# Fourier pieces placed in pairs between two feed-forward units, the second in a bank of u and v

## The chip, the cores and the metric

The kernel runs on one core of a Trainium2 chip. The metric is device time in microseconds (us) for one launch; the time before is the median of three runs. One further run was profiled, and every instruction time below is from that execution, counted from the start of its span.

## What is computed

```python
X = np.fft.fft(x, axis=1)          # x: 8 x 3008 x 256
X = np.fft.fft(X, axis=2)
x = X.real.reshape(8 * 3008, 256)
h = x @ w_in                       # 256 -> 2048
g = np.where(h >= 1, h, np.where(h <= -1, 0, (h + 1) ** 2 / 4))
return g @ w_out                   # 2048 -> 256
```

The weights arrive as 64-bit floats, so the kernel also converts them on the chip, at its start.

## The kernel before

The eight batches are taken one after the other. The 3008 points of a batch are 47 times 64, so its transform along the first axis is done in two stages of small matmuls. The transform along the second axis is folded into `w_in`. Because the input is real, outputs come in mirrored pairs, and the kernel computes for each pair two sums u and v, whose sum and difference are the two hidden values.

**Units.** The feed-forward part of a batch is 48 units: 3 chunks of up to 512 columns (482 in the first chunk) times 16 slices of the 2048 hidden features. `units` lists them; below, r is the number of a unit in its batch, 0 to 47. A unit i has two halves:

- `gemm1(i)`: three matmuls into a first bank (u) and three into a second (v), all on L344. Then VectorE forms `us` from u (L347), which is the last reader of u's bank, and `h = us - v` and `h = us + v` (L349, L350), which are the only readers of v's bank. Then come two ScalarE passes `a` (L353, L354), a VectorE pass over `h` (L355), a ScalarE rounding `gh` (L358) and two GpSimd differences `gl` (L360).
- `gemm2(i)`: twelve matmuls into four accumulators (L385) from `gh` and `gl`. It is issued `LAG` = 4 units behind `gemm1`. At the last slice of a chunk the accumulators are copied out by VectorE (L397) and ScalarE (L395), and the next chunk reuses the same four banks.

**PSUM.** The eight banks have fixed tags: four `acc`, three `uv` and one `fft`. A unit takes two `uv` banks, so three banks turn round: unit i has a and b, unit i+1 has c and a, unit i+2 has b and c.

**Pieces.** While batch b runs its 48 units, the transform of batch b+1 is done in 15 pieces: eight of `stage1` (L267: eight matmul records of 96 columns, the first piece two more from L270), one `nyquist` (L282: two records) and six of `stage2` (L303: eight records of 128 columns). Every piece writes a bank from `fft_bank`, which is the one bank with the tag `fft` (for batch 0, before the loop, the accumulators' banks are used instead). The bank is free again when it has been copied out: by four ScalarE copies `z` for `stage1` (L275), by ScalarE and VectorE (L169, L170) for `stage2`. `stage1` of piece q needs `y`, a GpSimd sum of two halves of the input (L131), with three buffers.

**Where pieces stand.** The loop over units calls `gemm1(i)`, then possibly a piece, then `gemm2(i - LAG)`. A piece is due when the share of the work done has fallen behind the share of units passed (`done < total * ...`), and in any case at the first slice of a chunk (`change`). It is held back one unit before such a change (`soon`). From batch 1 on this puts the 15 pieces behind the units r = 0, 4, 6, 9, 13, 16, 20, 23 (`stage1`), 26 (`nyquist`), 28, 31, 34, 36, 41 and 44 (`stage2`). For batch 0 they stand between r = 25 and 46. The last batch has none.

**Order.** Tile buffers and semaphores come from the framework. Its scheduler lays down, when the kernel is built, one fixed order of instructions for each engine. That order starts from the program's, but an instruction whose buffer or input is not expected in time is passed by others.

Of the kernel before, what the change touches and what calls it, by code (L numbers as in the profile page):

```python
# [9 lines left out]
F32 = mybir.dt.float32  # L10
# [12 lines left out]
P = 128  # L23
XC = 8
GPC = 4
CH = 512
# [83 lines left out]
def fft_ffn_kernel(ctx: ExitStack, tc: tile.TileContext, x, cst, w_in, w_out, out):  # L110
# [5 lines left out]
    ps = ctx.enter_context(tc.tile_pool(name="ps", bufs=1, space=bass.MemoryType.PSUM))  # L116
# [3 lines left out]
    def load_x(b, q):  # L120
        tag, bufs = ("xt", 4) if b or q < 4 else ("gl", 4) if q < 7 else ("o", 2)
        t = sb.tile([96, 2, CH], F32, tag=tag, name=f"x_{b}_{q}", bufs=bufs)
        nc.sync.dma_start(t, x[b, q])
        xt[b, q] = t
# [31 lines left out]
    def load_cm():  # L156
        nc.sync.dma_start(cm, cst[:, _OFF[3] :])

    early = [0]

    def fft_bank(b, name):

        if b == 0 and early[0] < EARLY_BANKS:
            early[0] += 1
            return ps.tile([P, CH], F32, tag=f"acc{early[0] % 4}", name=name, bufs=1)
        return ps.tile([P, CH], F32, tag="fft", name=name, bufs=1)

    def split(hi, lo, src):
# [23 lines left out]
    def convert_w(n):  # L192
# [3 lines left out]
        if n in CV:  # L196
            tag, bufs = CV[n]
            t = sb.tile([P, 2, CH], U32, tag=tag, name=f"cv_{n}", bufs=bufs)
            man, exp = t[:, 0], t[:, 1]
            lowf, shifted = low.bitcast(F32), exp  # L200
        else:
            if n % 2 == 0:
                f32s["pair"] = sb.tile([P, 2, CH], U32, tag="xt", name=f"cv_{n}", bufs=4)
            man, exp = f32s["pair"][:, n % 2], high
            lowf = fft_bank(1, f"cps_{n}")
            shifted = lowf.bitcast(U32)
# [28 lines left out]
    def fold_bank(f4, name):  # L235
        if f4 < 2:
            return fft_bank(0, name)
        return ps.tile([P, CH], F32, tag="uv", name=name, bufs=3)
# [69 lines left out]
    def fft_pieces(b):  # L308
        pieces = []
        for q in range(XC):  # L310
            pieces.append((4, lambda q=q: stage1(b, q)))
        pieces.append((2, lambda: nyquist(b)))
        for h in range(NC // 4):
            pieces.append((4, lambda h=h: stage2(b, h)))
        return pieces
# [19 lines left out]
    def gemm1(i):  # L335
        b, k, f, *_ = units[i]
        n = WIDTH[k]
        hi, lo = pq[b, k]
        cols = slice(f * P, (f + 1) * P)
        uv = []  # L340
        for m in range(2):
            t = ps.tile([P, CH], F32, tag="uv", name=f"uv_{i}_{m}", bufs=3)
            for j, (w, r) in enumerate(((wh, hi), (wl, hi), (wh, lo))):
                nc.tensor.matmul(t[:, :n], w[m][:, cols], r[:, m, :n], start=(j == 0), stop=(j == 2))  # L344
            uv.append(t[:, :n])
        us = sb.tile([P, CH], F32, tag="us", name=f"us_{i}", bufs=2)[:, :n]
        nc.vector.scalar_tensor_tensor(us, nyb[b, k][:, :n], delta[:, f : f + 1], uv[0], op0=ALU.mult, op1=ALU.add)  # L347
        h = sb.tile([P, 2, CH], F32, tag="h", name=f"h_{i}", bufs=3)[:, :, :n]
        nc.vector.tensor_tensor(h[:, 0], us, uv[1], op=ALU.subtract)  # L349
        nc.vector.tensor_tensor(h[:, 1], us, uv[1], op=ALU.add)  # L350
        a = sb.tile([P, 2, CH], F32, tag="a", name=f"a_{i}", bufs=3)[:, :, :n]

        nc.scalar.activation(a, h, AF.Relu, bias=half, scale=0.5)  # L353
        nc.scalar.activation(a, a, AF.Square)  # L354
        nc.vector.scalar_tensor_tensor(h, a, 1.0, h, op0=ALU.min, op1=ALU.max)  # L355
        gh = sb.tile([P, 2, CH], F32R, tag="gh", name=f"gh_{i}", bufs=4)[:, :, :n]
        gl = sb.tile([P, 2, CH], F32R, tag="gl", name=f"gl_{i}", bufs=4)[:, :, :n]
        nc.scalar.activation(gh, h, AF.Copy)  # L358
        for sg in range(2):
            nc.gpsimd.tensor_tensor(gl[:, sg], h[:, sg], gh[:, sg].bitcast(F32), op=ALU.subtract)  # L360
        acts[i] = gh, gl

    accs = []
    per = NCHUNK * NFT
    n_units = NB * per

    def gemm2(i):
        b, k, f, first, last, (v, visits) = units[i]
        n = WIDTH[k]
        gh, gl = acts.pop(i)  # L370
        if first:
            accs[:] = [ps.tile([P, CH], F32, tag=f"acc{j}", name=f"acc_{i}_{j}", bufs=1) for j in range(4)]
            if v:

                outs[k] = new_o(i)
                for dh in range(2):
                    nc.sync.dma_start(outs[k][dh][:, :, :n], parts[k][dh, :, :, :n])
        if last:
            o = outs.pop(k) if v else new_o(i)
        for dh in range(2):  # L380
            wc = slice(dh * P, (dh + 1) * P)
            for sg in range(2):
                acc = accs[dh * 2 + sg]
                for j, (w, g) in enumerate(((woh, gh), (wol, gh), (woh, gl))):
                    nc.tensor.matmul(  # L385
                        acc[:, :n], w[:, f, wc], g[:, sg], start=(first and j == 0), stop=(last and j == 2)
                    )
                if last:

                    dst = o[dh][:, sg, :n]  # L390
                    with tc.high_priority(offset=EVICT_AHEAD):
                        if v:
                            nc.vector.tensor_tensor(dst, acc[:, :n], dst, op=ALU.add)
                        elif sg:
                            nc.scalar.activation(dst, acc[:, :n], AF.Copy)  # L395
                        else:
                            nc.vector.tensor_copy(dst, acc[:, :n])  # L397
                    if i == n_units - 1:
                        nc.sync.dma_start(out[b, k, dh, sg, :, :n], dst)
            if last and v < visits - 1:  # L400
                nc.sync.dma_start(parts[k][dh, :, :, :n], o[dh][:, :, :n])
            elif last and i < n_units - 1:
                nc.sync.dma_start(out[b, k, dh].rearrange("s p t -> p s t")[:, :, :n], o[dh][:, :, :n])
# [7 lines left out]
    n1 = XC  # L411
# [11 lines left out]
    def run_steps(names):  # L423
        for s in names.split():
            steps[s[0]](int(s[1:]))
# [3 lines left out]
    pending, done, total = [], 0, 1  # L429
    for i in range(n_units + LAG):  # L430
        run_steps(STEPS.get(i, ""))
        if i < n_units:
            b, r = divmod(i, per)
            r0 = 0 if b else FIRST_DFT
            if r == (0 if b else FIRST_LOAD) and b + 1 < NB:
                for q in range(4):
                    load_x(b + 1, q)
            if r == r0:
                pending = fft_pieces(b + 1) if b + 1 < NB else []
                done, total = 0, sum(w for w, _ in pending)  # L440
            gemm1(i)

            change = units[max(i - LAG, 0)][3]
            soon = units[max(i - LAG + 1, 0)][3]
            while pending and (change or not soon and done < total * (r + 1 - r0) / (per - r0)):
                change = False
                w, f = pending.pop(0)
                f()
                done += w
                k1 = n1 + 7 - len(pending)  # L450
                if 4 <= k1 + 3 < XC:
                    load_x(b + 1, k1 + 3)
        if i >= LAG:
            gemm2(i - LAG)

# [53 lines left out]
```

## Time and profile before

| | |
|---|---|
| median of 3 runs | 1774.29 us (1773.91 to 1776.93) |
| profiled run | 1774.87 us, of which 1773.1 us are the span of the trace |
| granted TensorE clock, mean | 0.995 |
| matmuls into `acc` / `uv` | 4608 / 2304 |
| one evacuation copy `z` on ScalarE | 339 ns, 256 of them |
| the fold `y` on GpSimd | 1789 ns, 56 of them |

The span is the time from the first to the last instruction in the trace; the run's own time lies 1.8 us above it. In the trace, PE is TensorE's matmuls, PEld its weight loads, DVE is VectorE, ACT is ScalarE and POOL is GpSimd. A matmul is in flight longer than its turn: matmuls overlap, so what a matmul costs is the distance from its start to the next start, not its duration. Each row of a timeline gives start, duration, engine, line, operation and tiles, and at its end in brackets the idle time of the engine before it and what ended it.

### The profile page before, as it was taken

What the parts mean: (1) busy time and instruction counts of PE and PEld (TensorE: products, weight loads), DVE (VectorE), ACT (ScalarE), POOL (GpSimd) and SP (SyncE); (2) the same over time, 40 slices, a digit from 0 to 9 for tenths busy, and PEclk for the clock granted to TensorE, in tenths of its full rate; (3) what the DMA queues carried; (4) which work ended last, traced back from release to release, by engine and by line L of the source; (5) the groups of instructions that cost most, each with busy time, mean ns of one, the idle gap of its engine ahead of it and who ended that gap; (6) DMA issues with size and microseconds to landing.
All of it is one profiled execution on the core that took longest, in us unless ns stands there. A gap on an engine that the chain in (4) does not pass through costs nothing.

```text
span 1773.1 us, 21990 instructions
## 1 busy us (share of the span) xinstructions
PE 1743.6 (98%) x8014; PEld 1425.2 (80%) x8014; DVE 1439.3 (81%) x1762; ACT 1345.3 (76%) x1577; POOL 1199.4 (68%) x837
## 2 busy tenths in 40 slices
PE   9998999999999999999999999999999999999998
PEld 6766788888888788887888888888888888888876
DVE  5989888888887888878878788878888788888886
ACT  4776777787777777777778877788778787777775
POOL 0545776776677767687667776677666766667766
PEclk8999999999999999999999999999999999999999
DMA  7013322010011100101001100011000000000000
GB/s 228 1 58 111 100 82 89 28 50 18 24 43 30 58 31 1 51 27 53 30 10 51 49 28 24 19 41 50 28 25 33 1 23 33 10 24 12 12 25 24
DMA packets 29964, 72.53 MB, mean 41 GB/s; under 512 B 2976, under 2 KB 8224, under 8 KB 29856
## 3 DMA queue, kind: packets, MB, share of 16 engines
q1 hardware_dynamic: 29568, 70.08, 11.9%
q8 instruction: 63, 1.03, 0.2%
q10 hardware_dynamic: 288, 1.05, 0.2%
q14 instruction: 45, 0.37, 0.1%
HBM read 43.31 MB, written 27.81 MB: 40 GB/s over the span
## 4 chain that ended last, share of the span: by engine, by line
PE 70%; ACT 11%; DVE 7%; POOL 5%; issue 5%; DMA 1%; POOLq 0%; ACTq 0%; DVEq 0%
PE acc L385 43%; PE uv L344 22%; POOL gl L360 5%; DVE h L355 5%; ACT a L354 4%; ACT gh L358 3%; ACT a L353 3%; PE s L267 2%; PE s L303 2%; ACT z L275 1%; DMA raw<-in_moe_w_in_dram 1%; PE wps L246 1%; DVE h L349 0%; DVE h L350 0%; DVE o L397 0%
## 5 line engine op out<-in xcount | busy, mean ns | idle before, releaser
L360 POOL TENSOR_TENSOR gl<-h,gh 128x512 fp32r<-128x512 f32 (+1 forms) x768 | 1099.1, 1454 | 539.6 <-ACT gh L358 517.3
L355 DVE SCALAR_TENSOR_TENSOR h<-a,h 128x1024 f32<-128x1024 f32 (+1 forms) x384 | 581.6, 1514 | 226.0 <-ACT a L354 224.4
L358 ACT ACTIVATE gh<-h 128x1024 fp32r<-128x1024 f32 (+1 forms) x384 | 400.6, 1043 | 356.3 <-DVE h L355 327.5
L385 PE MATMUL acc<-gh,woh 128*128 128x512 f32 (+1 forms) x1536 | 608.5, 397 | 7.4 <-ACT gh L358 4.1
L385 PE MATMUL acc<-gl,woh 128*128 128x512 f32 (+1 forms) x1536 | 604.7, 394 | 6.8 <-POOL gl L360 6.7
L385 PE MATMUL acc<-gh,wol 128*128 128x512 f32 (+1 forms) x1536 | 596.8, 389 | 0.5 <-DVE wol L170 0.5
L353 ACT ACTIVATE a<-h,biases 128x1024 f32<-128x1024 f32 (+1 forms) x384 | 431.6, 1124 | 12.2 <-DVE h L350 9.8
L354 ACT ACTIVATE a<-a 128x1024 f32<-128x1024 f32 (+1 forms) x384 | 398.5, 1038 | 7.1
L385 PEld LDWEIGHTS acc<-gl,woh 128*128 128x128 f32 x1536 | 288.7, 188 | 74.1 <-POOL gl L360 14.5
L385 PEld LDWEIGHTS acc<-gh,woh 128*128 128x128 f32 x1536 | 289.7, 189 | 70.7 <-ACT gh L358 6.8
L385 PEld LDWEIGHTS acc<-gh,wol 128*128 128x128 f32 x1536 | 289.8, 189 | 60.8 <-DVE wol L170 1.3
L349 DVE TENSOR_TENSOR h<-us,uv 128x512 f32<-128x512 f32 (+1 forms) x384 | 259.6, 676 | 63.3 <-POOL gl L360 22.3
L344 PE MATMUL uv<-pqh,wh 128*128 128x512 f32 (+1 forms) x768 | 303.8, 396 | 4.5 <-DVE h L350 2.7
L344 PE MATMUL uv<-pql,wh 128*128 128x512 f32 (+1 forms) x768 | 301.9, 393 | 0.0
L344 PE MATMUL uv<-pqh,wl 128*128 128x512 f32 (+1 forms) x768 | 299.7, 390 | 0.0
L347 DVE SCALAR_TENSOR_TENSOR us<-nyb,delta,uv 128x512 f32<-128x512 f32 (+1 forms) x384 | 278.7, 727 | 15.9 <-PE uv L344 15.4
L350 DVE TENSOR_TENSOR h<-us,uv 128x512 f32<-128x512 f32 (+1 forms) x384 | 256.3, 668 | 0.0
L344 PEld LDWEIGHTS uv<-pqh,wh 128*128 128x128 f32 x768 | 144.4, 188 | 43.3 <-DVE h L350 8.5
L344 PEld LDWEIGHTS uv<-pql,wh 128*128 128x128 f32 x768 | 144.7, 188 | 32.5 <-issue 0.5
L344 PEld LDWEIGHTS uv<-pqh,wl 128*128 128x128 f32 x768 | 144.5, 188 | 30.1
L131 POOL TENSOR_TENSOR y<-x 96x512 f32<-96x512 f32 x56 | 100.1, 1789 | 7.1 <-PE s L267 3.1
L275 ACT ACTIVATE z<-s 64x192 f32<-64x192 f32 x256 | 86.8, 339 | 14.0 <-PE s L267 6.7
(53 smaller groups left out, 552.5 us busy)
## 6 DMA issues: line engine op xcount, KB each, us to landing
x<-in_x_dram SPq DMA_DIRECT2D x64, 384.0 KB, 3.3
out_dram<-o SPq DMA_DIRECT2D x30, 512.0 KB, 2.8
out_dram<-o SPq DMA_DIRECT2D x16, 482.0 KB, 3.1
nyb<-nyr SPq DMA_DIRECT2D x24, 256.0 KB, 3.3
raw<-in_moe_w_out_dram SPq DMA_DIRECT2D x8, 512.0 KB, 11.7
raw<-in_moe_w_in_dram SPq DMA_DIRECT2D x6, 512.0 KB, 5.2
part<-o SPq DMA_DIRECT2D x4, 512.0 KB, 3.5
o<-part SPq DMA_DIRECT2D x4, 512.0 KB
```

What stands on the lines that cost most here:

```text
L131: nc.gpsimd.tensor_tensor(y, t[:, 0], t[:, 1], op=ALU.add)
L275: nc.scalar.activation(dst, src, AF.Copy)
L344: nc.tensor.matmul(t[:, :n], w[m][:, cols], r[:, m, :n], start=(j == 0), stop=(j == 2))
L347: nc.vector.scalar_tensor_tensor(us, nyb[b, k][:, :n], delta[:, f : f + 1], uv[0], op0=ALU.mult, op1=ALU.add)
L349: nc.vector.tensor_tensor(h[:, 0], us, uv[1], op=ALU.subtract)
L350: nc.vector.tensor_tensor(h[:, 1], us, uv[1], op=ALU.add)
L353: nc.scalar.activation(a, h, AF.Relu, bias=half, scale=0.5)
L354: nc.scalar.activation(a, a, AF.Square)
L355: nc.vector.scalar_tensor_tensor(h, a, 1.0, h, op0=ALU.min, op1=ALU.max)
L358: nc.scalar.activation(gh, h, AF.Copy)
L360: nc.gpsimd.tensor_tensor(gl[:, sg], h[:, sg], gh[:, sg].bitcast(F32), op=ALU.subtract)
L385: nc.tensor.matmul(acc[:, :n], w[:, f, wc], g[:, sg], start=(first and j == 0), stop=(last and j == 2))
```

## The change

Where one piece was due, two are now placed, one directly behind the other. `fft_bank` gives the first of the two the `fft` bank as before and the second a bank of the tag `uv`. The test for a due piece is the same, but it is asked once for a unit instead of in a loop, and a due unit places two pieces whether or not the second is due. The input loads that follow a piece go with it. The number of banks and buffers stays the same.

```diff
-    early = [0]
+    early, second = [0], [False]
...
             return ps.tile([P, CH], F32, tag=f"acc{early[0] % 4}", name=name, bufs=1)
+        if second[0]:
+            return ps.tile([P, CH], F32, tag="uv", name=name, bufs=3)
         return ps.tile([P, CH], F32, tag="fft", name=name, bufs=1)
...
-            while pending and (change or not soon and done < total * (r + 1 - r0) / (per - r0)):
-                change = False
-                w, f = pending.pop(0)
-                f()
-                done += w
-                k1 = n1 + 7 - len(pending)
-                if 4 <= k1 + 3 < XC:
-                    load_x(b + 1, k1 + 3)
+            if pending and (change or not soon and done < total * (r + 1 - r0) / (per - r0)):
+
+                for second[0] in (False, True):
+                    if pending:
+                        w, f = pending.pop(0)
+                        f()
+                        done += w
+                        k1 = n1 + 7 - len(pending)
+                        if 4 <= k1 + 3 < XC:
+                            load_x(b + 1, k1 + 3)
+                second[0] = False
```

With the weights 4, 2 and 4 of the pieces, the same test now gives pairs behind r = 0, 4, 13 and 20 (two `stage1` each), 26 (`nyquist` and the first `stage2`), 31 and 36 (two `stage2` each), and the last `stage2` alone behind r = 44. In batch 0 the pairs stand behind r = 25, 28, 31, 34, 36, 40 and 44, with the last piece behind 46.

## The prediction

> **What bounds the kernel now.** I read the page's busy times and chain of waits first.
>
> ```profile
> span 1773.1 us, 21990 instructions
> ...
> PE 1743.6 (98%) x8014; PEld 1425.2 (80%) x8014; DVE 1439.3 (81%) x1762; ACT 1345.3 (76%) x1577; POOL 1199.4 (68%) x837
> ...
> PE 70%; ACT 11%; DVE 7%; POOL 5%; issue 5%; DMA 1%; POOLq 0%; ACTq 0%; DVEq 0%
> ```
>
> TensorE is busy for 98% of the span and holds most of the chain. An average over stages says little, so next I asked for busy times by stage; the columns are the stretch, its length, then each engine's busy time.
>
> ```profile
> 100.00:200.00 100.00, 87.97 (x382) 65.59 (x381) 90.30 (x125) 73.33 (x95) 59.23 (x45) 1.00 0.29 92
> ...
> 496.00:584.00 88.00, 88.00 (x419) 74.50 (x418) 69.42 (x82) 69.09 (x89) 64.66 (x47) 1.00 0.12 39
> ...
> 285.00:1557.00 1272.00, 1270.86 (x5898) 1052.06 (x5897) 1031.79 (x1230) 988.66 (x1146) 907.72 (x627) 1.00 0.10 32
> ```
>
> From 285 to 1557 us, the steady stretch of six batches with all their pieces, the PE row shows 1.1 us of idle in 1272. The idle time of the kernel lies at its start, while weights are converted (12 us of idle between 100 and 200), and in the last batch, which has no pieces. So the change can win in the steady stretch only by making matmul turns shorter, or by removing short waits that a busy row hides. Those are in the view of waits, from 285 to 1557 us (total, times, longest), for matmuls:
>
> ```profile
> PE acc L385 <- DVE o L397: 0.8, 3, 0.3
> ```
>
> and for their weight loads, which wait in a matmul's place:
>
> ```profile
> PEld uv L344 <- DVE h L350: 3.7, 11, 0.5
> PEld acc L385 <- DVE o L397: 3.1, 5, 0.7
> PEld uv L344 <- DVE us L347: 2.3, 7, 0.4
> ```
>
> Two kinds of wait exist: 3.9 us on the copies that empty the accumulators at a change of chunk, and 6.0 us on VectorE to give back a bank of u and v. The second kind is small, but it shows that the `uv` banks are already used to the edge.
>
> **The change part by part.**
>
> *Turns of the matmuls.* No matmul is removed. What pairing can save is the passage from a piece back to the units. A `stage1` piece looks so on PE:
>
> ```profile
> 553.75 1.03 PE L267 MATMUL s<-cs,y 96*128 96x96 f32 x8
> 554.57 0.46 PE L385 MATMUL acc<-gh,woh 128*128 128x482 f32 x1
> 554.87 0.38 PE L385 MATMUL acc<-gh,wol 128*128 128x482 f32 x1
> 555.09 0.38 PE L385 MATMUL acc<-gl,woh 128*128 128x482 f32 x1
> ```
>
> A `stage2` piece, in a chunk of 512 columns:
>
> ```profile
> 435.70 1.05 PE L303 MATMUL s<-cs,z 128*128 128x128 f32 x8
> 436.51 0.48 PE L385 MATMUL acc<-gh,woh 128*128 128x512 f32 x1
> 436.82 0.39 PE L385 MATMUL acc<-gh,wol 128*128 128x512 f32 x1
> 437.05 0.39 PE L385 MATMUL acc<-gl,woh 128*128 128x512 f32 x1
> ```
>
> And `nyquist`:
>
> ```profile
> 611.65 0.31 PE L282 MATMUL ny<-cs,z 128*24 128x64 f32 x2
> 611.90 0.51 PE L385 MATMUL acc<-gh,woh 128*128 128x512 f32 x1
> 612.24 0.39 PE L385 MATMUL acc<-gh,wol 128*128 128x512 f32 x1
> ```
>
> The `stage1` piece takes 554.57 - 553.75 = 0.82 us, and the first matmul behind it keeps PE 0.30 us instead of the 0.22 of the next one: 0.90 us for eight records, 0.112 each. The `stage2` piece takes 0.81 + (0.31 - 0.23) = 0.89 us, 0.111 each. In flow, eight records at about 0.11 are 0.88 us anyway, so one passage less is worth at most 0.02 us there. `nyquist` takes 0.25 + (0.34 - 0.23) = 0.36 us for two records (0.23 as in the rows before); joined to the piece behind it, it can come down to two turns of 0.11, a gain of about 0.14 us. I give the same to the pair of r = 0, whose first piece ends with two short records. Per batch that is 0.14 + 0.14 + 5 x 0.02 = 0.4 us, in seven batches 2.7 us. That is the whole direct gain.
>
> *Accumulators at a change of chunk.* At r = 20 one piece stands in front of the first matmuls into the emptied accumulators, and it does not cover the copies quite:
>
> ```profile
> 586.16 0.39 PE L385 MATMUL acc<-gl,woh 128*128 128x512 f32 x1
> 586.81 0.50 PE L385 MATMUL acc<-gh,woh 128*128 128x512 f32 x1 [0.27 <-DVE o L397]
> ```
>
> The step is 0.65 us where 0.23 is usual: 0.42 us lost. A second piece adds 0.9 us of cover. The waits of this kind come to 3.9 us in the steady stretch. They go whole if the copies keep their place, and not at all if the added ScalarE copies push the accumulators' copies back. I take 2 us.
>
> *The bank.* This is the term that is not in the trace of before. In r = 13 of batch 2 the piece above ends at 554.57. A second piece moves all that follows on PE by about 0.9 us. The next two units stand on PE like this (first and fourth matmul of the second one shown):
>
> ```profile
> 558.38 0.38 PE L344 MATMUL uv<-pql,wh 128*128 128x482 f32 x1
> 558.60 0.38 PE L385 MATMUL acc<-gh,woh 128*128 128x482 f32 x1
> ...
> 561.23 0.38 PE L344 MATMUL uv<-pqh,wh 128*128 128x482 f32 x1
> ...
> 561.89 0.38 PE L344 MATMUL uv<-pqh,wh 128*128 128x482 f32 x1
> ```
>
> VectorE in that time:
>
> ```profile
> 560.14 0.70 DVE L347 SCALAR_TENSOR_TENSOR us<-nyb,delta,uv 128x482 f32<-128x482 f32 x1
> 562.60 1.40 DVE L355 SCALAR_TENSOR_TENSOR h<-a,h 128x964 f32<-128x964 f32 x1 [1.76 <-ACT a L354]
> 563.93 0.64 DVE L349 TENSOR_TENSOR h<-us,uv 128x482 f32<-128x482 f32 x1
> 564.49 0.65 DVE L350 TENSOR_TENSOR h<-us,uv 128x482 f32<-128x482 f32 x1
> ```
>
> And ScalarE's copies of the single piece:
>
> ```profile
> 558.75 1.04 ACT L275 ACTIVATE z<-s 64x192 f32<-64x192 f32 x3
> ...
> 562.59 0.34 ACT L275 ACTIVATE z<-s 64x192 f32<-64x192 f32 x1
> ```
>
> The four copies of a single piece are fitted in between other work and end at 562.93, 8.4 us behind the piece. A second piece's four stand behind them: 4 x 0.34 more, so its `uv` bank is not free before about 564.3. Until then the units turn round two banks. The unit at 561.23, moved to 562.1, gets u's bank in time (`us` of the unit before ends at 560.84). For v, at 562.8, it needs either the bank that the `h` at 564.49 gives back at 565.14, or the piece's own at 564.3. That is 1.5 to 2.3 us late. With three banks the same matmul needed only the `us`.
>
> What this costs depends on what stands next in PE's queue. Twelve `acc` matmuls are at hand there, 561.23 - 558.60 = 2.63 us of work. If the scheduler puts them ahead of the three v matmuls, PE waits for nothing; if not, everything behind waits 1.5 to 2.3 us. The trace has a case of the first kind. In batch 0, two pieces were placed behind one unit (r = 44) with only the `fft` bank for both:
>
> ```profile
> 268.02 1.05 PE L303 MATMUL s<-cs,z 128*128 128x128 f32 x8
> ...
> 271.69 0.40 PE L344 MATMUL uv<-pqh,wh 128*128 128x512 f32 x1
> ...
> 272.39 1.05 PE L303 MATMUL s<-cs,z 128*128 128x128 f32 x8
> 273.20 0.48 PE L344 MATMUL uv<-pqh,wh 128*128 128x512 f32 x1
> ```
>
> The second piece stands 4.4 us behind the first, in the middle of the next unit's six matmuls, and no idle time is marked. So orders do bend round a missing bank. But they are fixed beforehand, and VectorE's wait of 1.76 us above shows that the engines do not meet as the order expects. I count a remainder of 0.1 us for each of 7 x 7 = 49 pairs, 5 us; the ends are 0 and, with 2 us for half of them, 50 us. The Trainium skill (Perfetto Trace Analysis, Optimizing Tensor Performance) says that independent matmul groups should rotate through different PSUM banks so that the emptying of one overlaps the next. By it the second piece is right to have a bank of its own, but the units lose theirs: the same rule speaks for and against. The same page (Identifying Performance Opportunities, Optimization Strategy) takes a repeating gap as a sign that there is not enough PSUM; no such gap is in the rows above, and by it one should appear behind the pairs.
>
> *What else moves.* The `y` sums and the input loads come earlier.
>
> ```profile
> L131 POOL TENSOR_TENSOR y<-x 96x512 f32<-96x512 f32 x56 | 100.1, 1789 | 7.1 <-PE s L267 3.1
> ```
>
> Three `y` buffers suffice for two pieces and for one sum ahead, and POOL has 73% load in the window of 496 to 584 us (64.66 of 88), so I cost them at nothing. The cover is the four units or more between two `stage1` pairs; where it failed, a pair would wait one sum, 1.8 us. In batch 0, from 170 to 285 us, pieces move between stalled units; I take 0, bounds 3 us either way.
>
> The sum, against the profiled run of 1774.87 us: -2.7 - 2 + 5 + 0 = +0.3, so 1775 us in that run's terms. The median stands 0.6 lower: 1774.6 us.
>
> **The rivals.**
>
> *Faster: the gains come and the bank costs nothing.* The order bends at every pair as at 272 us. Then -2.7 - 3.9 = -6.6, less up to 3 at the start: 1765 to 1770, at its middle 1768 us. For it speaks that PE always has twelve matmuls at hand. Against it that it needs every gain whole.
>
> *Slower: the two-bank stretch.* The mechanism is that of 562.8 above: v's bank comes back only with the second `h`, which VectorE does behind the L355 of the unit before. It decides as soon as the wait left over per pair passes (4.7 + 3.5) / 49 = 0.17 us. At 0.3 to 0.8 us for each of 49 pairs it costs 15 to 40, less the 4.7: 1784 to 1810 us, and nearest to the rows 1790, some 0.4 us a pair. For it speak the 6.0 us of waits on `uv` already there, and a bank that is held 8 us and more; against it the orders that bend.
>
> *The pair is not a pair.* If the scheduler finds no `uv` bank for the second piece, it drifts behind the next matmuls as at 272.39, and PE does the same work in another order: 1774 us, with neither gain nor loss.
>
> **How the numbers follow.** A difference under 0.2% (3.5 us) can't be told from no change here. The forecast, gains and bank costs nearly even, with the drifting pair, has 0.35 and its own range is 1771 to 1778. Faster has 0.30, slower 0.35. Range for 8 in 10: down to 1766, and up into the slower case to 1793, which leaves out its dearer end.
>
> **What would show it.** In the changed trace: the second piece at 0.11 us a record directly behind the first (the 2.7 us); no step of 0.65 us at r = 20 (the 2 us); the order of PE behind pairs, with `acc` matmuls between u's and v's three (bending) or weight loads and matmuls of `uv` waiting for L350 or L275 (the slower case), to be summed against 6.0 us. The forecast is wrong if those waits pass 12 us, or if ScalarE's eight copies make `gl` late, seen as `acc` waiting for L360.

## The result and the profile after

The changed kernel takes 1821.18 us (median of 4 runs, 1818.98 to 1822.49) against 1775.61 us: a ratio of 1.0255, with a 95% interval of 1.0242 to 1.0267. It is 2.5% slower. The profiled run took 1821.51 us, its span 1819.7 us.

The page of the changed kernel, its busy times and the chain of waits:

```profile
span 1819.7 us, 21986 instructions
...
PE 1760.3 (97%) x8014; PEld 1437.1 (79%) x8014; DVE 1454.0 (80%) x1762; ACT 1348.1 (74%) x1577; POOL 1188.4 (65%) x837
...
PE 61%; ACT 16%; DVE 10%; issue 3%; POOL 1%; ACTq 0%; POOLq 0%; DVEq 0%
```

In the chain, PE has lost 9 points and POOL 4, while ACT has won 5 and DVE 3. Lines are shifted by two against the kernel before: L344 became L346, L350 became L352, L355 became L357, L385 became L387. From the first `uv` matmul of one batch to that of the next, the batches with r = 0 to 47 and a full successor (the second to the sixth of eight) take 219.1 to 221.9 us instead of 210.4 to 212.1: 48 us more in five batches (one profiled run of each kernel). The first batch takes 246.0 instead of 245.8 us, the last 217.1 instead of 218.6. So the start plays no part in the loss. The seventh batch is the odd one: it has the same pairs, but only the last transform is left, so nothing is folded ahead behind its later pairs. It takes 213.0 instead of 210.9 us, only 2.1 more.

The waits of the changed kernel in its steady stretch (285 to 1600 us; total, times, longest), first of matmuls, then of weight loads:

```profile
PE uv L346 <- DVE us L349: 16.5, 10, 2.2
PE s L269 <- DVE h L352: 8.6, 10, 1.3
PE uv L346 <- ACT z L277: 8.2, 10, 1.0
```

```profile
PEld uv L346 <- DVE us L349: 21.8, 15, 2.6
PEld uv L346 <- ACT z L277: 12.8, 10, 1.4
PEld s L269 <- DVE h L352: 10.9, 12, 1.5
PEld ny L284 <- issue: 2.2, 6, 0.4
```

The matmuls wait 33 us, where the kernel before had 0.8. (The rows of weight loads are mostly the same waits seen from the other queue; they are not added.) Three things are waited for: `us`, which gives back u's bank; the second `h` (L352), which gives back v's bank and for which now the second piece itself waits; and the copies `z`, which give back the lent bank. The wait on the accumulators' copies is gone.

The largest single wait, 2.2 us, comes once in each of five batches, behind r = 21. There VectorE and GpSimd look so:

```profile
598.04 1.30 DVE L357 SCALAR_TENSOR_TENSOR h<-a,h 128x1024 f32<-128x1024 f32 x1 [0.30 <-ACT a L356]
600.53 4.80 DVE L357 SCALAR_TENSOR_TENSOR h<-a,h 128x1024 f32<-128x1024 f32 x1 [1.18 <-ACT a L356]
605.25 0.74 DVE L349 SCALAR_TENSOR_TENSOR us<-nyb,delta,uv 128x512 f32<-128x512 f32 x1
```

```profile
595.73 2.54 POOL L362 TENSOR_TENSOR gl<-h,gh 128x512 fp32r<-128x512 f32 x2
598.22 2.27 POOL L131 TENSOR_TENSOR y<-x 96x512 f32<-96x512 f32 x1
600.45 1.30 POOL L131 TENSOR_TENSOR y<-x 96x512 f32<-96x512 f32 x1
601.70 2.54 POOL L362 TENSOR_TENSOR gl<-h,gh 128x512 fp32r<-128x512 f32 x2
```

In the kernel before, one fold stands alone at this place, and the passes over `h` beside it are short:

```profile
589.93 2.28 POOL L131 TENSOR_TENSOR y<-x 96x512 f32<-96x512 f32 x1
```

```profile
589.73 1.32 DVE L355 SCALAR_TENSOR_TENSOR h<-a,h 128x1024 f32<-128x1024 f32 x1 [0.30 <-ACT a L354]
592.22 1.22 DVE L355 SCALAR_TENSOR_TENSOR h<-a,h 128x1024 f32<-128x1024 f32 x1 [0.51 <-ACT a L354]
```

In the changed kernel the pass over `h`, whose median is 1.46 us, takes 4.80 us. It starts 0.08 us after the second of two folds `y` that now stand side by side, and ends at 605.33, 1.1 us behind the end of the second `gl` (604.24). GpSimd works from 595.73 to 604.24 with no gap. The pass reads two operands in SBUF, `a` and `h`; in the kernel before, its longest was 2.80 us after 285 us. The Trainium skill (SBUF — State Buffer, Who interferes with whom) says that a VectorE instruction with two SBUF inputs and a GpSimd instruction that reads SBUF exclude each other, and that the later one is blocked until the first is done. The trace agrees that the pass stands still, but here not for one instruction: it was held through a fold and two `gl`. That is not the usual case. After 285 us, 146 passes of this trace begin while one GpSimd instruction runs and another is queued directly behind it; 135 of them wait for the running one alone and take at most 2.16 us, and 11 are held through more.

Two folds stand side by side at four places in a steady batch, behind the pairs of r = 0, 4, 13 and 20 (in the second batch not behind r = 4). Only the last two places stretch a pass over `h` beyond 3 us: in each of five batches to 3.40 us behind r = 13, which costs TensorE a wait of 0.8 to 1.4 us for `us`, and to 4.80 us behind r = 20. What makes these two places different from the first two was not tried.

TensorE at the place of the 4.80 us pass:

```profile
603.45 0.40 PE L387 MATMUL acc<-gl,woh 128*128 128x512 f32 x1
606.04 0.49 PE L346 MATMUL uv<-pqh,wh 128*128 128x512 f32 x1 [2.19 <-DVE us L349]
606.37 0.40 PE L346 MATMUL uv<-pqh,wl 128*128 128x512 f32 x1
606.61 0.45 PE L346 MATMUL uv<-pql,wh 128*128 128x512 f32 x1
607.96 0.79 PE L346 MATMUL uv<-pqh,wh 128*128 128x512 f32 x1 [0.90 <-ACT z L277]
```

And the same place by stretches (length, then busy times and counts of PE, PEld, DVE, ACT, POOL, the granted clock, DMA):

```profile
599.50:606.80 7.30, 5.11 (x22) 3.68 (x20) 6.14 (x4) 3.96 (x6) 4.97 (x5) 1.00 0.38 108
606.80:613.60 6.80, 5.90 (x14) 4.46 (x14) 3.68 (x6) 5.13 (x8) 3.00 (x3) 0.50 0.00 0
613.60:620.40 6.80, 6.80 (x30) 5.45 (x29) 4.23 (x6) 4.42 (x5) 2.65 (x3) 1.00 0.00 1
```

Behind the wait the granted clock falls to 0.50 for 6.8 us, in which TensorE starts 14 matmuls where the next stretch of the same length has 30. So the two folds seem to cost three times here: the late `us`, the late copies `z`, and the clock. The experiments test this.

### The profile page after: what moved, and what is told of

Read it like the earlier page. It is cut to its first block, busy times and chain, and to the rows that moved or that the text cites. A ratio compares the mean times of both kernels' runs of the same rounds, so it can differ in the third digit from the quotient of the medians.

```text
span 1819.7 us, 21986 instructions
## 1 busy us (share of the span) xinstructions
PE 1760.3 (97%) x8014; PEld 1437.1 (79%) x8014; DVE 1454.0 (80%) x1762; ACT 1348.1 (74%) x1577; POOL 1188.4 (65%) x837
## 4 chain that ended last, share of the span: by engine, by line
PE 61%; ACT 16%; DVE 10%; issue 3%; POOL 1%; ACTq 0%; POOLq 0%; DVEq 0%
PE acc L387 38%; PE uv L346 20%; DVE h L357 8%; ACT a L356 5%; ACT gh L360 4%; ACT a L355 4%; PE s L305 2%; ACT z L277 2%; POOL gl L362 1%; PE s L269 1%; DVE h L352 1%; DVE h L351 1%; DVE us L349 0%; DVE o L395 0%; DVE o L399 0%
## 5 line engine op out<-in xcount | busy, mean ns | idle before, releaser
L357 DVE SCALAR_TENSOR_TENSOR h<-a,h 128x1024 f32<-128x1024 f32 (+1 forms) x384 | 586.5, 1527 | 186.1 <-ACT a L356 183.3
L387 PE MATMUL acc<-gh,woh 128*128 128x512 f32 (+1 forms) x1536 | 608.7, 397 | 6.8 <-ACT gh L360 4.6
L387 PE MATMUL acc<-gl,woh 128*128 128x512 f32 (+1 forms) x1536 | 608.9, 396 | 6.0 <-POOL gl L362 6.0
L387 PE MATMUL acc<-gh,wol 128*128 128x512 f32 (+1 forms) x1536 | 601.4, 392 | 0.5 <-DVE wol L172 0.5
L355 ACT ACTIVATE a<-h,biases 128x1024 f32<-128x1024 f32 (+1 forms) x384 | 431.9, 1125 | 39.3 <-DVE h L352 36.6
L387 PEld LDWEIGHTS acc<-gl,woh 128*128 128x128 f32 x1536 | 291.9, 190 | 74.1 <-POOL gl L362 13.5
L387 PEld LDWEIGHTS acc<-gh,woh 128*128 128x128 f32 x1536 | 292.9, 191 | 68.6 <-ACT gh L360 6.8
L387 PEld LDWEIGHTS acc<-gh,wol 128*128 128x128 f32 x1536 | 292.7, 191 | 63.7 <-DVE wol L172 1.3
L346 PE MATMUL uv<-pqh,wh 128*128 128x512 f32 (+1 forms) x768 | 306.9, 400 | 27.7 <-DVE us L349 16.5
L346 PE MATMUL uv<-pql,wh 128*128 128x512 f32 (+1 forms) x768 | 304.0, 396 | 0.0
L346 PE MATMUL uv<-pqh,wl 128*128 128x512 f32 (+1 forms) x768 | 300.9, 392 | 0.0
L352 DVE TENSOR_TENSOR h<-us,uv 128x512 f32<-128x512 f32 (+1 forms) x384 | 256.3, 667 | 0.0
L346 PEld LDWEIGHTS uv<-pqh,wh 128*128 128x128 f32 x768 | 145.3, 189 | 69.9 <-DVE us L349 22.3
L346 PEld LDWEIGHTS uv<-pql,wh 128*128 128x128 f32 x768 | 145.7, 190 | 32.8 <-issue 0.5
L346 PEld LDWEIGHTS uv<-pqh,wl 128*128 128x128 f32 x768 | 145.5, 189 | 30.7
L131 POOL TENSOR_TENSOR y<-x 96x512 f32<-96x512 f32 x56 | 90.3, 1630 | 4.5 <-PE s L269 1.9
```

The costliest lines, as they stand in the source:

```text
L131: nc.gpsimd.tensor_tensor(y, t[:, 0], t[:, 1], op=ALU.add)
L387: nc.tensor.matmul(acc[:, :n], w[:, f, wc], g[:, sg], start=(first and j == 0), stop=(last and j == 2))
```

## The experiments

Two theories stood against each other. The **bank theory** says that a lent bank of u and v is what units and pieces wait for. The **fold theory** says that a pair sets two `y` buffers free at once, so that two folds stand in a row on GpSimd, hold up VectorE, and so stop TensorE. Each run below is compared with the kernel before on the same chip (1775 to 1776 us there).

| kernel | time, us | ratio to before, 95% |
|---|---|---|
| the change | 1821.2 | 1.0255 (1.0242 to 1.0267) |
| pairs, both in the `fft` bank | 1810.7 | 1.0203 (1.0188 to 1.0219) |
| single pieces, every second in a lent bank | 1785.6 | 1.0069 (1.0046 to 1.0093) |
| the change, folds apart | 1794.1 | 1.0106 (1.0089 to 1.0122) |
| only `nyquist` and `stage2` paired | 1782.7 | 1.0044 (1.0029 to 1.0059) |
| before, folds side by side | 1797.3 | 1.0129 (1.0105 to 1.0153) |
| folds apart, copies `z` sooner | 1800.0 | 1.0137 (1.0119 to 1.0156) |
| the change, no folds | 1770.7 | 0.9974 (0.9963 to 0.9986) |
| folds apart, second piece behind `gemm2` | 1790.4 | 1.0086 (1.0067 to 1.0104) |
| before, no folds | 1760.4 | 0.9919 (0.9904 to 0.9934) |
| the change, TensorE kept busy at r = 22 | 1815.2 | 1.0226 (1.0208 to 1.0245) |
| before, folds by the transfers | 1766.5 | 0.9944 (0.9930 to 0.9959) |
| the change, folds by the transfers | 1790.4 | 1.0077 (1.0060 to 1.0094) |

**Pairs without a lent bank.**

```diff
-        if second[0]:
-            return ps.tile([P, CH], F32, tag="uv", name=name, bufs=3)
```

> Pairs as in the change, but the second piece takes the fft bank too, so no bank of u and v is lent. Bank theory (units wait for a lent bank): the whole loss goes, 1772 to 1780 us, and no matmul of uv waits for L275-type copies. Fold theory (two GpSimd folds y run back to back and hold up VectorE's pass over h, whose lateness stops TensorE): the second piece waits for the one bank, so the two y buffers come free at different times; the folds should lie apart and the time be 1772 to 1785 us as well. This run alone does not tell the two apart; it shows whether pairing without the lent bank costs anything. If it stays above 1800 us, the bank is innocent.

1810.7 us, above the 1800 at which the text calls the bank innocent. That reading was too quick. The matmul waits are of another kind:

```profile
PE s L267 <- ACT z L275: 15.2, 12, 3.0
PE s L303 <- ACT nyt L284: 4.1, 5, 1.0
```

The second piece now waits for the first one's copies, up to 3.0 us, and no matmul of `uv` is among the waits. No pass over `h` takes more than 2.4 us after 285 us, so the loss is not the folds' doing. TensorE's order does bend: in five batches the second piece of the pair of r = 13 stands behind the `uv` matmuls of the next unit, and waits there 1.7 us all the same. The run shows that pairing without a second bank costs 36 us. It does not clear the lent bank.

**Lent bank without pairs.**

```diff
                 w, f = pending.pop(0)
+                second[0] = len(pending) % 2 == 1
                 f()
+                second[0] = False
```

> Pieces stand singly behind the units of before, but every second one takes a bank of u and v. Bank theory: a bank is lent as often as in the change, so most of the loss comes, 1800 to 1822 us. Fold theory: single pieces free one y buffer at a time, so GpSimd never runs two folds in a row, VectorE's pass over h stays under 3 us, and the time is 1774 to 1785 us.

1785.6 us, just above the fold theory's range and far under the bank theory's. All of the listed matmul waits are 9.2 us of pieces on the second `h`. Two folds never stand side by side after 285 us, and no pass over `h` takes more than 2.8 us. So a lent bank has a price of its own, about 10 us when pieces stand singly.

**The change with the folds apart.** The second of two folds is queued behind the last `gl` of the unit that the pair follows:

```diff
+            n = 8 * b + q
+            k = (n - 3) // 2 - 4
+            if n % 2 == 0 and 0 <= k < len(paired):
+                with tc.issue_after(last_gl[paired[k]]):
+                    nc.gpsimd.tensor_tensor(y, t[:, 0], t[:, 1], op=ALU.add)
```

> The change whole, with one edit: the second of the two folds that a pair of stage1 pieces sets free is queued on GpSimd behind the last gl of the unit that the pair follows, so that the two folds are two units apart. Bank theory: no effect, 1815 to 1825 us. Fold theory: no pass over h (4.80 us at five places in the change) over 3 us, no stretch of half clock behind r = 22, and 1780 to 1792 us; what is left over before, some 2 us a batch, is then the bank's.

1794.1 us: 27 us of the 46 are gone by moving one fold of each pair in GpSimd's queue, 2 us fewer than the expected range asks for. After 285 us no pass over `h` takes more than 2.4 us, and no stretch of half clock is left. What remains are 19 us, with these waits:

```profile
PE uv L353 <- ACT z L284: 8.1, 17, 1.0
PE s L276 <- DVE h L359: 6.1, 8, 1.1
```

Both are on the lent bank: the unit for the piece's copies, the piece for the unit's v.

**Pairs of `stage2` alone.**

```diff
-                    if pending:
+                    if pending and (not second[0] or len(pending) < 7):
```

> Only nyquist and the stage2 pieces are paired and lend the bank; stage1 pieces stand singly as before. Bank theory in its plain form (any lent bank costs 1 us or more): four lent banks a batch cost 20 to 30 us, 1795 to 1805 us. Fold theory: stage2 frees no y buffer, so 1770 to 1777 us. In the trace of the change TensorE has no wait over 0.2 us behind these pairs, so both would have to explain a loss here.

1782.7 us, between the two. The waits are 6.5 us of `uv` and 1.9 us of pieces, both on the second `h`, which gives back a bank of u and v. In the change these pairs showed no such wait, probably because the waits and the half clock behind r = 20 had just given VectorE time: where that half clock is taken away (the run on the clock below), 0.7 us of this wait come back in each of five batches. So even three pairs a batch, with no fold set free by them, cost 7 us, and the waits are on a bank.

**Folds side by side without pairs.** The reverse of the run before last: in the kernel before, the first of two folds is made to wait until the second can follow.

```diff
+            n = 8 * b + q
+            if n % 2 == 1 and n - 2 in placed:
+                with tc.issue_after(last_gl[placed[n - 2] - 2]):
+                    nc.gpsimd.tensor_tensor(y, t[:, 0], t[:, 1], op=ALU.add)
```

> The kernel before, single pieces, every piece in the fft bank, no bank lent; only the folds are queued so that two stand side by side on GpSimd, as in the change. Fold theory: passes over h (L355 of before) of 3.4 to 4.8 us come back, three or four a batch. If the folds alone suffice to stop TensorE, 1790 to 1805 us with stretches of half clock; if it also takes the lent bank (three banks of u and v have room for a late VectorE), under 1785 us. Bank theory: no effect, 1772 to 1778 us, however long the passes.

1797.3 us: side by side, the folds cost 22 us with every bank in its place. Two passes over `h` took 4.46 and 3.42 us in the second batch; after 500 us the long ones were shorter than expected, 2.6 to 3.2 us, and there was no half clock after 285 us. TensorE's waits:

```profile
PE uv L350 <- DVE h L356: 10.0, 10, 1.4
PE uv L350 <- DVE us L353: 2.5, 4, 0.9
```

GpSimd has the same block as the change has behind r = 20, fold, fold, `gl`, `gl`:

```profile
581.80 2.23 POOL L135 TENSOR_TENSOR y<-x 96x512 f32<-96x512 f32 x1
583.98 1.30 POOL L137 TENSOR_TENSOR y<-x 96x512 f32<-96x512 f32 x1
585.25 2.41 POOL L366 TENSOR_TENSOR gl<-h,gh 128x482 fp32r<-128x482 f32 x2
```

**Copies sooner.** From the kernel with the folds apart; `z` of `stage1` goes 150 places forward in the scheduler's order.

```diff
-                nc.scalar.activation(dst, src, AF.Copy)
+                with tc.high_priority(offset=EVICT_AHEAD if b else 0):
+                    nc.scalar.activation(dst, src, AF.Copy)
```

> The kernel with the folds apart (1794.1 us) with the four copies z of a stage1 piece moved 150 places forward in ScalarE's order, so that a lent bank comes back sooner. If the 8 us of waits of units on these copies are what is left of the loss, 1783 to 1788 us and those waits near 0. If ScalarE then delays its passes a and gh in turn, no gain or slower, 1794 to 1800 us.

1800.0 us, 6 us more and at the edge of the second range; the two ratios' intervals (1.0137 and 1.0106) just touch. Pieces wait 15.0 us on the second `h`, and units still wait 11.5 us on `z`: those at r = 6 are gone, those near r = 14 have grown from 0.5 to 1.7 us and more. The third to the sixth batch take 215.1 to 215.6 us, as with the folds apart (214.9 to 215.6). The surplus stands in the second batch (220.3 instead of 213.4 us), where two passes over `h` take 3.6 and 4.5 us although no two folds stand side by side, and in the seventh (215.5 instead of 212.9). So sooner copies won nothing; whether ScalarE's other passes lost by them is not shown.

**No folds.** `fold_x` hands `stage1` the first half of x for all batches but the first.

```diff
-            nc.gpsimd.tensor_tensor(y, t[:, 0], t[:, 1], op=ALU.add)
-            yt[b, q] = [y]
+            yt[b, q] = [t[:, 0]]
```

> The change, with the GpSimd sums y left out for all batches but the first: stage1 reads the first of the two halves alone, so its output is not the transform; every matmul, bank and copy stays. Fold theory: like the folds apart or better, 1783 to 1794 us, with no pass over h above 2.4 us. Bank theory in its strong form: 1810 us or more.

1770.7 us, less than the kernel before, with all pairs and lent banks in place; the output is not the transform. No pass over `h` is longer than 2.37 us in the whole run. This rules out the bank theory in its strong form, but it needed a measure of its own:

> The kernel before with the sums y left out in the same way (stage1 reads one half alone). It is the measure for the changed kernel without folds, 1770.7 us. If pairs with a lent bank cost nothing of their own once GpSimd has no folds, this takes 1768 to 1774 us as well. If it is under 1762 us, the pairs still cost 8 us or more and the folds' absence only paid for it.

The kernel before without folds takes 1760.4 us. So the folds cost the old kernel 15 us too, and pairs with a lent bank still cost 10 us where no fold disturbs (7.7 us over the second to the seventh batch of the two traces). That is the second of the two cases named, and the 1770.7 us alone would have misled.

**Second piece behind `gemm2`.** From the kernel with the folds apart.

```diff
                 for second[0] in (False, True):
+                    if second[0] and i >= LAG:
+                        gemm2(i - LAG)
```

> The kernel with the folds apart, with the second piece of a pair placed behind gemm2 instead of in front of it, so that its bank is due 2.7 us later. The 7.5 us of waits of the second piece on L352-type h should vanish; the units behind it then have the bank missing 2.7 us later as well. If the first is the larger, 1784 to 1790 us; if the waits only move to the units, 1792 to 1800 us.

1790.4 us, at the border of the two. The pieces' wait is gone, and the units' wait on `z` has doubled to 15.0 us. The 4 us between this run and the folds apart lie ahead of the second batch, which starts at 285.3 instead of 289.0 us; the second to the seventh batch together take 1286.8 instead of 1287.4 us. So the waits only move from the piece to the units, as a bank too few should have it.

**The clock.**

```diff
+            if r == 22 and 0 < b < NB - 2:
+                bank = fft_bank(b, f"fill_{b}")
+                for _ in range(10):
+                    nc.tensor.matmul(bank, wh[0][:, :P], wh[0][:, :CH], start=True, stop=True)
             gemm1(i)
```

> The change with ten matmuls more in front of the unit r = 22 of five batches, into the fft bank, whose result nothing reads: 2.1 us of work where TensorE waits 2.2 us for us. Their price in TensorE's order would be 10 us. If the half clock behind that wait (five stretches of 6.8 us, each 3.4 us of work lost) comes from the idle time, it goes, and the kernel with more work is faster: 1803 to 1812 us and a mean clock of 0.995. If the clock falls for another reason, 1820 to 1832 us.

The kernel with fifty matmuls more is 6 us faster, 1815.2 (1811.8 to 1817.6) against 1821.2 us (1819.0 to 1822.5); their ratios' intervals just touch. The ten matmuls stand where the wait was, and the clock stays up:

```profile
600.74 2.45 PE L446 MATMUL fill<-wh 128*128 128x512 f32 x10
603.12 0.49 PE L346 MATMUL uv<-pqh,wh 128*128 128x512 f32 x1
```

```profile
604.00:611.00 7.00, 6.04 (x27) 4.77 (x27) 4.05 (x6) 4.61 (x7) 3.40 (x3) 1.00 0.00 0
```

So the half clock comes from the idle time: no stretch of it is left after 180 us and before the end. The 4.8 us passes over `h` are still there. The gain is smaller than expected, 6 us instead of 9 to 18. A likely reason is that the slow stretch had given the other engines time: without it, new waits stand behind r = 26 (3.4 us of `uv` on the second `h`).

**Folds by the transfers.** The first half of x is loaded as before, and a GpSimd-queue transfer adds the second half on the way in, for seven of eight sums of a batch.

```diff
-        nc.sync.dma_start(t, x[b, q])
+        if b and q:
+            nc.sync.dma_start(t[:, 0], x[b, q][:, 0])
+            nc.gpsimd.dma_start(t[:, 0], x[b, q][:, 1], accum_op=ALU.add)
+        else:
+            nc.sync.dma_start(t, x[b, q])
```

> The kernel before with seven of the eight sums y of a batch taken off GpSimd's adder: the first half of x is loaded as before and the second is added to it by the transfer itself (a GpSimd-queue DMA that accumulates). Single pieces, nothing lent. If what the folds cost is the time in which GpSimd's reads hold up VectorE, this comes near the kernel before without folds, 1760 to 1768 us. If GpSimd is held as long by issuing the transfers, or the adding transfers land late, 1775 to 1790 us.

1766.5 us, ratio 0.9944 (0.9930 to 0.9959): faster than both kernels. The second line is the kernel before, in the same stretch (columns as above):

```profile
285.00:1550.00 1265.00, 1264.30 (x5886) 1051.85 (x5885) 1027.21 (x1228) 987.28 (x1145) 854.25 (x624) 1.00 0.12 33
285.00:1550.00 1265.00, 1263.86 (x5867) 1046.34 (x5866) 1026.00 (x1223) 983.88 (x1141) 904.45 (x625) 1.00 0.10 32
```

TensorE's busy time is the same within 0.5 us, but 19 matmuls more start in it. From the third batch to the seventh each takes 210.4 us, the same as in the kernel without folds; the kernel before takes 210.9 to 212.1 there.

The same in the change:

> The change with the same sums done by transfers. If the large part of its loss is the two folds in a row, it comes near the change without folds, 1770 to 1780 us, with one fold (q = 0) a batch left on GpSimd and no stretch of half clock after 300 us. If the loss is the lent bank whatever GpSimd does, 1800 us or more.

1790.4 us, a miss by 10 us. No pass over `h` takes more than 2.8 us after 285 us, yet 24 us stay over the same kernel with single pieces, with these waits:

```profile
PE s L275 <- DVE h L358: 10.5, 10, 1.8
PE uv L352 <- ACT z L283: 3.7, 8, 0.6
```

The half clock is not gone either: it stands for 3.4 us behind r = 20 in four batches. It decides little of the loss, since the fifth batch, without it, takes as long (215.6 us) as its neighbours (215.2 and 214.6).

**What the runs say together.** Set by folds and by placing, the times make a cross (us):

| | folds one at a time | folds side by side | no folds | folds by transfers |
|---|---|---|---|---|
| single pieces, no bank lent | 1775 | 1797 | 1760 | 1766 |
| pairs, second in a lent bank | 1794 | 1821 | 1771 | 1790 |
| difference | 19 | 24 | 10 | 24 |

Neither theory holds alone. Pairs with a lent bank cost 10 to 24 us, 19 with the folds set apart. Two folds side by side cost 22 us without and 27 us with the pairs. Measured apart from each other the two are 19 and 22 us, 41 of the 46 that the change loses by doing both. The sum hides something: over the second to the seventh batch of the traces alone, the two cost 18.9 and 17.9 us, and both together 50.3. So some 13 us belong to neither alone. The half clock is a part of them (6 us by the run that kept TensorE busy). That the rest comes where a late VectorE meets a missing bank is likely, but was not shown. Why the lent bank costs 10 us without folds and 24 with folds by transfers was not tried further; the waits only show that it is the second `h` that comes late in the dear case.

## Why the prediction was wrong

- *What bounds the kernel.* TensorE has almost no idle time in the steady stretch, as read. That there was little to win does not follow from it: the kernel before with the folds by transfers is 10 us faster at the same busy time. The 6.0 us of waits on `uv` were named for the slower rival, but no term of the sum was made of them.
- *Turns of the matmuls (2.7 us won).* Wrong, nothing came. `nyquist` with a `stage2` piece behind it, and a pair of `stage1`, in the changed kernel:

```profile
628.18 0.31 PE L284 MATMUL ny<-cs,z 128*24 128x64 f32 x2
628.42 1.16 PE L305 MATMUL s<-cs,z 128*128 128x128 f32 x8
629.34 0.48 PE L387 MATMUL acc<-gh,woh 128*128 128x512 f32 x1
629.66 0.40 PE L387 MATMUL acc<-gh,wol 128*128 128x512 f32 x1
```

```profile
784.22 1.92 PE L269 MATMUL s<-cs,y 96*128 96x96 f32 x16
785.93 0.46 PE L387 MATMUL acc<-gh,woh 128*128 128x482 f32 x1
786.23 0.38 PE L387 MATMUL acc<-gh,wol 128*128 128x482 f32 x1
```

The first pair costs 629.66 - 628.18 - 0.23 = 1.25 us, exactly the 0.36 + 0.89 of the two alone. The second costs 2.01 - 0.22 = 1.79 us, twice 0.90. The pair of r = 0 costs 2.21 us, again the sum of its two pieces. So pairing saved nothing in any of the three.

- *Accumulators (2 us won).* Right in kind: the row of `acc` waiting for the copies is gone in the changed kernel. What that saved by itself was not measured.
- *The bank (5 us lost).* Mis-sized. The step that failed is "orders do bend round a missing bank" with its remainder of 0.1 us a pair. Behind the pairs of `stage1` the changed kernel keeps six `uv` and twelve `acc` matmuls in turn, as before, and TensorE waits behind r = 4, 13 and 20. Measured with the folds apart the term is 19 us, 0.4 us for each of 49 pairs, which is what the slower rival had put: 1790 us against 1794. One wait has no term in the sum: the second piece itself waits for its bank (8.6 us), since that is given back only by the second `h` of the unit before. The prediction let a piece without a bank drift behind other matmuls for nothing.
- *What else moves (0).* This step failed as well, and it put the time far outside the range. The `y` sums were costed "at nothing" by a load of 73% on GpSimd and a deadline four units away. Neither was the point. The sums were in time: no matmul waits for a `y` after 285 us. But two of them in a row held up VectorE's pass over `h`, and that costs 22 us alone, and 27 on top of the pairs, in which the half clock has a part (6 us by the run that filled the wait). The bank's cost alone, 1794 us, would have stood 1 us above the range's upper end of 1793; so the bank's term brings the time to the edge, and the folds carry it to 1821.

The prediction's own sign came true in its size: it was to be wrong if the waits of `uv`, 6.0 us before, passed 12 us, and they are 24.7 us among the matmuls alone. But 16.5 of these are on `us` and none on the second `h` that it had named.

## What to carry to other kernels

A load below 100% does not make an engine free: where two engines exclude each other, ask how long the one works without a gap, for so long the other may stand. A busy row at 100% does not mean that nothing is to be won either: count the matmuls that start in it. An edit that frees two buffers at once lets their refills run back to back somewhere else, so follow each freed buffer to the engine that fills it. And a bank lent out of a ring is paid for at both ends, by the borrower waiting for it and by the owner missing it.

## What the hardware showed unexpectedly

- A VectorE pass with two SBUF operands took 4.80 us instead of 1.3 to 1.5, held by three GpSimd instructions in a row, in all five batches within 0.02 us of the same length. Of the passes that met a queue on GpSimd in this trace, 135 of 146 were held by one instruction only.
- Waits of TensorE of 2.2 us, followed by one of up to 1.0 us, brought the granted clock to 0.50 for 6.8 us, five times of five. In the change with folds by transfers, waits of 1.5 to 1.8 us at r = 20 brought it down for 3.4 us in four batches of five. The length of a wait alone does not decide it: with the copies sooner, a wait of 2.24 us left the clock at 1.00.
- Fifty matmuls that compute nothing made the kernel 6 us faster by keeping that clock.
